# Cosine attention and an MLP mixer on one core: two row sums move from VectorE to GpSimd, and one block of queued matmuls is queued a slot later

## The chip, the cores and the metric

The kernel runs on one NeuronCore of a Trainium2 chip. The core has a matrix engine (TensorE; PE for its matmuls and PEld for its weight loads in the profile), VectorE (DVE), ScalarE (ACT), GpSimd (POOL) and SyncE (SP, which here only issues DMAs). Each engine runs its own instructions in the order in which the program lists them, and waits for the others through semaphores. The metric is the device time of one execution in microseconds (us); lower is better.

## The reference

Eight batches of attention over normalised queries and keys, and then, on the attention's output x, a token mixer and a channel mixer:

```python
# q, k, v: (8, 12, 448, 64)
q_n = q / (norm(q) + 1e-6);  k_n = k / (norm(k) + 1e-6)
attn = softmax(q_n @ k_n.T / tau)            # per batch and head, 448 x 448
x = (attn @ v)                               # -> (8, 448, 768)
h = relu(x.T @ w_tok1) @ w_tok2              # 448 -> 256 -> 448, over tokens
u = x + h.T
h2 = relu(u @ w_ch1) @ w_ch2                 # 768 -> 1536 -> 768, over channels
out = u + h2
```

## The kernel before, in words

**The main loop.** Twelve heads are taken in pairs, six pairs to a batch, so there are 48 pairs, numbered i = 0 to 47. One turn of the loop, called slot i here, carries several pairs at different stages: the scores and exponentials of pair i (`score`, L345, L352), the product with v of pair i-1 (`pv_rest`, `pv`, L367, L384, with the normalisation on VectorE, L387 and L388), the first token layer of pair i-1 (`tok1`, L420, its relu on VectorE, L423), the second token layer of pair i-2 (`tok2`, L434, its residual sum u on VectorE, L437) and the transposing DMA of that u into `ut` (`udma`, L443). The same slot casts v of pair i on GpSimd (`cast_v`, L228, L230), scales q and k of pair i+2 there (L298, L306), and sends them through a transposing DMA into `qk` (L330), all DMAs from SyncE's queue, in the program's order. An instruction that waits in a queue holds everything behind it.

**The channel layers are filler.** The channel mixer of the batches that are done is cut into units: one first-layer unit is six matmuls (`m_ch1`, L467, profile name psG; a batch has twelve), one second-layer unit is twelve matmuls (`m_ch2`, L483, psF). `refill(b)` appends a batch's units to a list; each slot adds an allowance (`fed[1]`, set by `RATES`) and takes units off the front until the allowance is used: one unit between `pv` and `score_rest`, the rest after `tok2`. For batch 5 (`KEPT_B`) the twelve first-layer units are put at the **front** of the list. Before the change that happens in slot 38, so that slot 38 takes two units of batch 5's first layer, slots 39 and 40 three each, slots 41 and 42 two each, and the unit of batch 4's second layer that stood at the front (psF of batch 4, block 0, second half) is taken in slot 42. A first-layer unit of batch 5 reads the transposed u of all six pairs of that batch, 30 to 35; u of pair 35 is made and sent in slot 37.

**The end is computed another way.** The second layer of batch 5 and both channel layers of batches 6 and 7 are left to the end and done with a seven-product scheme for 2 x 2 blocks (Strassen's, in Winograd's form). It needs sums and differences of blocks. Those of w_ch1 are `fast_weights1` (1 = s1w, 2 = s2w, 4 = s4w in the profile; 3 is written over a part of wc1t); s2w needs s1w, s4w needs s2w. Those of w_ch2 are `fast_weights2` (t1w, t2w, t3w, t4w, three parts each). Those of the activations are `fast_x` (t1x to t4x) for the first layer and `fast_g(g, k)` for the second, where g is one of five groups of rows and k = 1 to 4: the row sums S1 = G21 + G22 and S2 = S1 - G11, and so on. Group 0 is made of rows of batch 5 alone, so that its S1 and S2 (s1g and s2g) can be made before the loop ends. All of these are plain two-input fp16 operations (L536). S1 and S2 of group 0 are read first by `fast_g(0, 4)` and by the products `q5(0)` and `q6(0)` after the whole first layer.

**Where they stand before.** In slot 45 (NP_ALL - 3) VectorE's queue has, behind the relu of `tok1`, s1g and s2g, and behind these the reciprocals and products that finish the attention of pair 45 (`x`, L388). GpSimd's queue has in slot 46 the cast of v, s1w and t2w part 0; in slot 47 the cast of v, t2w part 1 and s4w; and then t4x's last part and t2w part 2. After the loop VectorE has `fast_weights1(3)` (wc1t, L536), t1x, then the sum u of pair 46 (L437).

Of the kernel before, what the change touches and what calls it, by code (L numbers as in the profile page):

```python
# [22 lines left out]
def kernel(  # L23
# [12 lines left out]
    nc = tc.nc  # L36

    B, H, S, E = q.shape
# [9 lines left out]
    NPAIR = H // 2  # L48
    NP_ALL = B * NPAIR
# [49 lines left out]
    def old(i):  # L99
        return i < OLD  # L100
# [167 lines left out]
    def norms(i, a0=0, a1=2, dve=False):  # L268
        st = pipe[i]
        n, sl = some(i, a0, a1)  # L270
        rn = st["rn"][0:n, sl]
        ne = nes[i % 3][0:n, sl]
        if dve:
            nc.vector.tensor_reduce(out=rn, in_=ne, axis=AXX.X, op=ALU.add)
            nc.vector.reciprocal(out=rn, in_=rn)  # L275
            return
        nc.scalar.activation(out=rn, in_=st["ssq"][0:n, sl], func=AF.Ln, bias=tiny[0:n])
        nc.scalar.activation(out=ne[:, :, 0], in_=rn, func=AF.Exp, scale=0.5)
# [59 lines left out]
    def score(i, c):  # L338
        n = SC if old(i) else 128
        qk = pipe[i]["qk"].rearrange("p a c s -> p (a c s)")  # L340
        qm = pipe[i]["qk"][:, 1, :, 0:SC]
        psS = ps2.tile([128, 2, 512], FP32, name=f"psS_{i}_{c}", tag="s")
        for hh in range(2):
            hb = slice(hh * 64, hh * 64 + 64)
            nc.tensor.matmul(psS[:, hh, 0:S], qk[hb, c * n:c * n + 128], qm[hb], start=True, stop=True)  # L345
        nc.scalar.activation(out=pts[i % 2][0:n, 2 * S * c:2 * S * (c + 1)].rearrange("p (h s) -> p h s", h=2),  # L346
                             in_=psS[0:n, :, 0:S], func=AF.Exp, scale=inv_tau)
# [77 lines left out]
    def tok2(i, pe=False, wide=False):  # L425
        st = pipe[i]
        b, pj = i // NPAIR, i % NPAIR
        if pj == 0:
            u16[b] = mix.tile([128, DT, 4, 128], FP16, name=f"u16_{b}", tag="u16", bufs=4)
            ut[b] = mix.tile([128, DT, 4, 128], FP16, name=f"ut_{b}", tag="ut")  # L430
        psU = (ps2 if wide else ps).tile([128, 4, 128], FP32, name=f"psU_{i}", tag="s" if wide else "b")
        for m, lo in enumerate(windows(b)):
            for tt in range(TT):
                nc.tensor.matmul(psU[:, m], w2t[:, tt, lo:lo + 128], st["rt"][:, tt],  # L434
                                 start=(tt == 0), stop=(tt == TT - 1))
        u = u16[b][:, pj]
        nc.vector.tensor_tensor(out=u, in0=psU[:], in1=st["x"][:], op=ALU.add)  # L437
        if not pe:
            udma(i)
# [5 lines left out]
    def upose(i, n=1):  # L445
        b, pj = i // NPAIR, i % NPAIR
        psT = ps.tile([128, n, 4, 128], FP16, name=f"psT_{i}", tag="b")
        for j in range(n):
            for m in range(4):
                nc.tensor.transpose(psT[:, j, m], u16[b][:, pj + j, m], id16[:])  # L450
        nc.vector.tensor_copy(out=ut[b][:, pj:pj + n], in_=psT[:])


    def upose_act(i, wide=False):
        psT = (ps2 if wide else ps).tile([128, 4, 128], FP16, name=f"psT_{i}", tag="s" if wide else "b")
        for m in range(4):
            nc.tensor.transpose(psT[:, m], u16[0][:, i, m], id16[:])
        nc.scalar.activation(out=ut[0][:, i], in_=psT[:], func=AF.Copy)
# [73 lines left out]
    KEPT_B = B - 3  # L532
    fw = {}

    def tt(eng, out, a, b, op):
        eng.tensor_tensor(out=out, in0=a, in1=b, op=op)  # L536
# [15 lines left out]
    def fast_weights1(n, eng):  # L552
        s, w = fw["s"], w1part
        out, a, b, op = {1: (s[0], w(1, 0), w(1, 1), ALU.add), 2: (s[1], s[0], w(0, 0), ALU.subtract),
                         3: (w(1, 0), w(0, 0), w(1, 0), ALU.subtract), 4: (s[2], w(0, 1), s[1], ALU.subtract)}[n]
        tt(eng, out if n == 3 else out[:], a[:] if n == 2 else a, b[:] if n == 4 else b, op)
# [87 lines left out]
    def fast_weights2(n, parts=range(3)):  # L644
        def w(i, j):
            return [wc2t[:, HC * i + 2 * m:HC * i + 2 * m + 2, DH * j:DH * (j + 1)] for m in range(3)]

        t = fw.setdefault("t2", {})
        if n not in t:
            at = [(n - 1 + m) % 2 for m in range(3)]  # L650
            t[n] = [qkv.tile([128, 2, DH], FP16, name=f"t{n}w2_{m}", tag=("qf", "kf")[z]) for m, z in enumerate(at)]
        a, b = {1: (w(0, 1), w(0, 0)), 2: (w(1, 1), t.get(1)), 3: (w(1, 1), w(0, 1)), 4: (w(1, 0), t.get(2))}[n]
        for m in parts:
            tt(nc.gpsimd, t[n][m][:], a[m], b[m] if n % 2 else b[m][:], ALU.subtract)
# [11 lines left out]
    def gtile(t, i):  # L666
        g, at = (gts["new"], t - 3) if 3 <= t < 7 else (gts[KEPT_B // 2], t if t < 3 else t - 3)
        return g[:, HC * i:HC * (i + 1), 128 * at:128 * at + 128]

    def s_tile(g, k):  # L670
        if g == 0 and k < 3:
            return qkv.tile([128, HC, 128], FP16, name=f"s{k}g_0", tag=("qf", "kf")[k - 1])[:]
        if g % 2:
            return xtile(k, f"g_{g}", [128, HC, 128])[:]
        n, part = (2, k - 3) if g == 0 else (1, k - 1) if k < 4 else (2, 4 - g)
        if n not in fw["room"]:
            fw["room"][n] = room(n, [128, 3, HC, 128], FP16)
        return fw["room"][n][:, part]

    def fast_g(g, k):  # L680
        r1, r2 = TILES[g]
        s = sg.setdefault(g, {})
        s[k] = s_tile(g, k)
        a, b, op = {1: lambda: (gtile(r2, 0), gtile(r2, 1), ALU.add),
                    2: lambda: (s[1], gtile(r1, 0), ALU.subtract),
                    3: lambda: (gtile(r1, 0), gtile(r2, 0), ALU.subtract),
                    4: lambda: (gtile(r1, 1), s[2], ALU.subtract)}[k]()
        tt(nc.vector, s[k], a, b, op)

    def prod2(n, g, out, start, lo=0, hi=DH):  # L690
        r1, r2 = TILES[g]
# [90 lines left out]
        return queue and fed[0] > queue[0][0] / 2  # L782

    KEPT = 6000.0
    RATES = {2 * NPAIR + 2: 4350.0, NP_ALL - 10: 3200.0}
    ACT_SQ = range(NP_ALL - 10, NP_ALL - 3)

    def refill(b):
# [7 lines left out]
    with tc.manual_schedule():  # L796
# [145 lines left out]
        for i in range(NPAIR + 1, NP_ALL):  # L942
            b, pj = i // NPAIR, i % NPAIR
            for c in range(KC):
                score(i, c)
                if c == 1 and NP_ALL - 6 <= i < NP_ALL - 2:
                    norms(i + 2)
            if i == NPAIR + 1:
                upose(i - 4, 2)
                tok2(i - 2, pe=True)  # L950
                pv_wide(i - 1)
                upose_act(i - 2)
                x_wide(i - 1)
                sums(i + 2)
            else:
                pv_rest(i - 1)
                pv(i - 1, 0)
                pv(i - 1, 1)
            if i == NP_ALL - 1:
                fast_weights1(2, nc.vector)  # L960
            if i == NPAIR + 1:
                refill(0)
            elif pj == 2 and 1 < b < B - 1:
                refill(b - 1)
            side(i)
            fed[1] = RATES.get(i, fed[1])
            if i == NP_ALL - HP:
                fed[1] = (sum(t for t, _ in queue) - fed[0]) / HP
            fed[0] += fed[1]
            unit(True)  # L970
            if old(i):
                score(i, KC)
            else:
                score_rest(i)
            if i in ACT_SQ:
                square(i + 3, 1, act=True)
            if i > NPAIR + 1:
                tok2(i - 2)
            if i + 1 < DMA_T0:
                tpose(i + 1)  # L980
            if due():
                unit(True)
            while due():
                unit()
            tok1(i - 1)
            if i + 3 < NP_ALL:
                sums(i + 3)
            if NP_ALL - 6 <= i < NP_ALL - 3:
                fast_weights2(1, (i - NP_ALL + 6,))
            if i == NP_ALL - 3:  # L990
                fast_g(0, 1)
                fast_g(0, 2)
                early.close()
                tail = ctx.enter_context(tc.tile_pool(name="tail", bufs=1, side="right", reuse_waits="tile"))
                tail_tiles()
            if i == NP_ALL - 2:
                fast_weights1(1, nc.gpsimd)
                fast_weights2(2, (0,))
            if i == NP_ALL - 1:
                fast_weights2(2, (1,))  # L1000
                fast_weights1(4, nc.gpsimd)
        last = NP_ALL - 1
        while queue:
            unit(True)
# [94 lines left out]
        g = n - 1  # L1099
# [46 lines left out]
```

## Time and profile before

| what | value |
|---|---|
| time, three runs | 394.35, 396.0, 394.37 us; median 394.37 |
| the profiled execution's own time | 392.86 us |
| its span, first to last instruction | 391.1 us |
| mean granted TensorE clock | 0.985 |
| matmuls of the first channel layer (L467) | 432, 89.5 us busy |
| matmuls of the second channel layer (L483) | 432, 76.2 us busy |
| s1w and s4w on GpSimd (128 x 2304, fp16) | 4.54 us each |
| t1w, t2w, t3w, t4w, one part (128 x 768, fp16) | 1.63 to 1.64 us where nothing is in the way |
| s2g on VectorE (128 x 768, fp16) | 0.56 us |
| s2w and wc1t on VectorE (128 x 2304, fp16) | 1.35 us each |

A page of the profile shows one execution: busy time of each engine, the span in forty slices, and the chain of work that ended last, followed back from the last instruction to what released each one. A line of the chain or of a timeline reads: start in us from the span's beginning, length in us, engine, what it writes, line of the program, how many. In timelines the form out<-in with shapes follows, and in square brackets the engine's idle time before and what ended it. A VectorE or GpSimd instruction's length includes time in which it has been issued and cannot proceed; a wait for a semaphore shows as idle time before it.

### The profile page before, as it was taken

Reading aid. Unit: us, or ns where it says so; the run is one execution under the profiler, and the core shown is the slowest. Engines: PE = TensorE matmul, PEld = TensorE weight load, DVE = VectorE, ACT = ScalarE, POOL = GpSimd, SP = SyncE. Lnnn points to the kernel's source line nnn. Section 1 sums busy time; section 2 is a strip of 40 time slices with the busy share of each in tenths; the row PEclk is TensorE's granted clock in tenths of the full one; section 3 lists DMA queues with packets and bytes.
Section 4 is the critical chain, followed back from the end, with each engine's and each line's share of the span. In section 5 each row is a group of like instructions: output and inputs, shape, how many; then the busy total and the mean of one; then the engine's idle time right before and its main releaser. Section 6 shows DMA issues by size and latency. Waiting matters only on the chain.

```text
span 391.1 us, 10297 instructions
## 1 busy us (share of the span) xinstructions
PE 367.7 (94%) x4074; PEld 240.6 (62%) x4074; DVE 260.6 (67%) x567; ACT 238.0 (61%) x412; POOL 288.0 (74%) x415
## 2 busy tenths in 40 slices
PE   7788999999999999999999999979999579999993
PEld 6466666676666666667667666646666356556662
DVE  7789866675646674566536675446667978797872
ACT  5999877665774456844866448758877324355110
POOL 8999988878767667668677667654789914797752
PEclk9999999999999999999999999999999959999999
DMA  7999999969997979767988899658797602103244
GB/s 211 278 226 241 260 228 217 178 147 220 208 213 141 215 171 213 172 151 193 186 204 142 208 195 209 163 136 154 183 176 156 109 13 55 22 0 91 82 139 105
DMA packets 118064, 64.65 MB, mean 165 GB/s; under 512 B 74240, under 2 KB 114560, under 8 KB 118016
## 3 DMA queue, kind: packets, MB, share of 16 engines
q1 hardware_dynamic: 111984, 58.42, 68.0%
q0 software_dynamic: 5616, 5.21, 8.5%
q8 instruction: 32, 0.52, 0.6%
q10 hardware_dynamic: 416, 0.36, 0.3%
q14 instruction: 16, 0.13, 0.1%
HBM read 43.45 MB, written 11.01 MB: 139 GB/s over the span
## 4 chain that ended last, share of the span: by engine, by line
PE 83%; DVE 6%; DMA 6%; ACT 1%; POOL 1%; issue 1%; SPq 0%; DVEq 0%; POOLq 0%
PE psG L467 20%; PE psF L483 18%; PE psO L384 9%; PE psS L345 7%; PE psU L434 5%; PE psR L420 5%; PE psYo L695 4%; DMA qf<-in_q_dram 3%; PE psY L590 3%; PE psZo L695 2%; PE psXo L695 2%; DVE s1g L536 2%; DMA kf<-in_k_dram 2%; PE psX L590 2%; PE psZ L590 2%; PE psQ L352 2%
## 5 line engine op out<-in xcount | busy, mean ns | idle before, releaser
L346 ACT ACTIVATE pt<-psS 128x896 f16<-128x896 f32 (+1 forms) x156 | 132.8, 916 | 57.6 <-PE psS L345 57.5
L467 PE MATMUL psG<-ut,wc1t 128*128 128x448 f16 x432 | 89.5, 352 | 2.4 <-DMA ut<-u 2.4
L298 POOL TENSOR_TENSOR kq<-kf,rn 128x384 f16<-128x384 f32 (+1 forms) x47 | 41.8, 890 | 62.4 <-DVE rn L275 58.8
L483 PE MATMUL psF<-wc2t,gt 128*128 128x384 f16 x432 | 76.2, 328 | 0.0
L467 PEld LDWEIGHTS <-wc1t 128*128 128x128 f16 x432 | 39.7, 98 | 31.0
L266 DVE TENSOR_REDUCE ssq<-sq 128x15 f32<-128x960 f32 (+2 forms) x51 | 56.1, 1101 | 2.9 <-ACT sq L248 1.9
L470 ACT ACTIVATE gt<-psG 128x448 f16<-128x448 f32 x72 | 38.7, 538 | 28.3 <-PE psG L467 28.3
L483 PEld LDWEIGHTS <-gt 128*128 128x128 f16 x432 | 40.7, 98 | 24.7 <-issue 0.7
L298 POOL TENSOR_TENSOR kq<-qf,rn 112x512 f16<-112x512 f32 x45 | 47.0, 1044 | 3.0
L423 DVE TENSOR_SCALAR rt<-psR 128x256 f16<-128x256 f32 x48 | 20.0, 418 | 41.7 <-PE psR L420 41.6
L345 PE MATMUL psS<-qk 64*128 64x448 f16 x312 | 42.4, 361 | 3.9 <-DVE qk L324 3.0
L487 DVE TENSOR_TENSOR ost<-psF,u 128x384 f32<-128x384 f32 (+1 forms) x42 | 22.8, 542 | 29.6 <-PE psF L483 29.4
L250 POOL TENSOR_TENSOR sq<-kf 128x384 f32<-128x384 f32 (+1 forms) x46 | 40.1, 873 | 0.0
L384 PE MATMUL psO<-vt,pt 128*128 128x65 f16 (+1 forms) x1024 | 39.7, 195 | 0.0
L434 PE MATMUL psU<-rt,w2t 128*128 128x128 f16 x384 | 29.8, 221 | 7.8 <-DVE x L388 7.3
L384 PEld LDWEIGHTS <-pt 128*128 128x128 f16 (+1 forms) x1024 | 34.7, 98 | 3.5 <-issue 0.9
L388 DVE TENSOR_TENSOR x<-psO,rec 128x256 f16<-128x256 f32 x82 | 34.8, 424 | 2.8
L437 DVE TENSOR_TENSOR u<-psU,x 128x512 f16<-128x512 f32 x48 | 32.2, 670 | 4.8 <-PE psU L434 3.5
L434 PEld LDWEIGHTS <-w2t 128*128 128x128 f16 x384 | 25.0, 99 | 15.6 <-DVE x L388 7.7
L250 POOL TENSOR_TENSOR sq<-qf 112x512 f32<-112x512 f32 x32 | 33.2, 1039 | 0.0
L420 PEld LDWEIGHTS <-w1t 128*128 128x128 f16 x384 | 25.2, 99 | 7.9 <-issue 1.8
L420 PE MATMUL psR<-x,w1t 128*128 128x128 f16 x384 | 29.8, 221 | 0.2 <-DVE u L437 0.2
(139 smaller groups left out, 532.1 us busy)
## 6 DMA issues: line engine op xcount, KB each, us to landing
qf<-in_q_dram SPq DMA_DIRECT2D x47, 224.0 KB, 4.2
kf<-in_k_dram SPq DMA_DIRECT2D x36, 192.0 KB, 3.9
vf<-in_v_dram SPq DMA_DIRECT2D x36, 192.0 KB, 3.6
vf<-in_v_dram SPq DMA_DIRECT2D x12, 224.0 KB, 7.6
kf<-in_k_dram SPq DMA_DIRECT2D x11, 224.0 KB, 7.8
wc1t<-in_moe_w_ch_dram POOLq DMA_DIRECT2D x4, 576.0 KB, 10.4
wc2t<-in_moe_w_ch_dram POOLq DMA_DIRECT2D x2, 1152.0 KB, 12.2
out_dram<-ost SPq DMA_DIRECT2D x5, 336.0 KB, 3.4
```

Source lines behind the costliest of these rows:

```text
L250: nc.gpsimd.tensor_mul(out=dst, in0=src, in1=src)
L266: nc.vector.tensor_reduce(out=st["ssq"][0:n, sl], in_=st["sq"][0:n, sl], axis=AXX.X, op=ALU.add)
L298: eng.tensor_tensor(out=kq[0:p, a, 0:n].rearrange("p c g e -> p g c e"), in0=st["kq"[a]][:].rearrange("p (g c) e -> p g c e", g=2), in1=_b ...
L345: nc.tensor.matmul(psS[:, hh, 0:S], qk[hb, c * n:c * n + 128], qm[hb], start=True, stop=True)
L346: nc.scalar.activation(out=pts[i % 2][0:n, 2 * S * c:2 * S * (c + 1)].rearrange("p (h s) -> p h s", h=2), in_=psS[0:n, :, 0:S], func=AF.Ex ...
L384: nc.tensor.matmul(psO[:, m, 0:E + 1], pts[i % 2][0:n, at:at + 128], vt[0:n, i % HP, nch * hh + c, 0:E + 1], start=(old(i) and c == 0), st ...
L388: nc.vector.tensor_tensor(out=st["x"][:, :, hh * E:(hh + 1) * E], in0=psO[:, :, 0:E], in1=_bcast_free(rec[:], E), op=ALU.mult)
L420: nc.tensor.matmul(psR[:, tt], w1t[:, w1[m], tt * 128:(tt + 1) * 128], st["x"][:, m], start=(m == 0), stop=(m == 3))
L434: nc.tensor.matmul(psU[:, m], w2t[:, tt, lo:lo + 128], st["rt"][:, tt], start=(tt == 0), stop=(tt == TT - 1))
L467: nc.tensor.matmul(psG[:, 0:S], wc1t[:, dt, ct * 128:(ct + 1) * 128], ut[b][:, dt].rearrange("p m s -> p (m s)")[:, lo:lo + S], start=(dt ...
L470: nc.scalar.activation(out=gt[:, ct, (b % 2) * S:(b % 2 + 1) * S], in_=psG[:, 0:S], func=AF.Relu)
L483: nc.tensor.matmul(psF[:, 0:hi - lo], gt[:, ct, at:at + 128], wc2t[:, ct, lo:hi], start=(ct == 0), stop=(ct == CT - 1))
```

## The change

Three edits. The first-layer units of batch 5 are put to the front of the list in slot 39 in place of 38, and the allowance per slot from 38 on is 3100 in place of 3200. `fast_g` takes an engine, and S1 and S2 of group 0 go to GpSimd, in slot 47, between the last cast of v and s4w. Part 0 of t2w moves from slot 46 to slot 45, and part 1 from before s4w to behind it.

```diff
-    def fast_g(g, k):
+    def fast_g(g, k, eng=nc.vector):
...
-        tt(nc.vector, s[k], a, b, op)
+        tt(eng, s[k], a, b, op)
...
-    RATES = {2 * NPAIR + 2: 4350.0, NP_ALL - 10: 3200.0}
+    RATES = {2 * NPAIR + 2: 4350.0, NP_ALL - 10: 3100.0}
...
-            elif pj == 2 and 1 < b < B - 1:
+            elif pj == (3 if b - 1 == KEPT_B else 2) and 1 < b < B - 1:
                 refill(b - 1)
...
             if i == NP_ALL - 3:
-                fast_g(0, 1)
-                fast_g(0, 2)
+                fast_weights2(2, (0,))
                 early.close()
...
             if i == NP_ALL - 2:
                 fast_weights1(1, nc.gpsimd)
-                fast_weights2(2, (0,))
             if i == NP_ALL - 1:
+                fast_g(0, 1, nc.gpsimd)
+                fast_g(0, 2, nc.gpsimd)
+                fast_weights1(4, nc.gpsimd)
                 fast_weights2(2, (1,))
-                fast_weights1(4, nc.gpsimd)
```

With the new allowance the list is taken off as follows (G is a first-layer unit of batch 5, F a second-layer unit of batch 4): before, slots 38 to 43 take 2 G, 3 G, 3 G, 2 G, 2 G + F, F; after, F, 3 G, 3 G, 2 G, 3 G, G + F. From slot 44 on both take the same units. The two stores of F's rows to memory move with it on SyncE's queue, from behind slot 42 to behind slot 38. GpSimd's order at the end becomes: scaling of pair 47, t2w part 0, cast, s1w, cast, s1g, s2g, s4w, t2w part 1, t4x's last part, t2w part 2; from there on it is as before.

## The prediction

> **What bounds the kernel now.** I read the page's engine shares first, then the chain of waits in order of time, then the two places where the chain leaves TensorE late in the run.
>
> ```profile
> PE 367.7 (94%) x4074; PEld 240.6 (62%) x4074; DVE 260.6 (67%) x567; ACT 238.0 (61%) x412; POOL 288.0 (74%) x415
> ...
> 256.85 1.00 DVE ssq L266
> 257.85 3.46 DMA ut<-u
> 262.34 1.14 PE psG L467 x6
> ...
> 301.38 1.95 PE psF L483 x12
> 305.02 9.43 DVE s1g L536
> 315.64 1.03 PE psU L434 x8
> ```
>
> TensorE is the bound, so only its idle time and its clock are to be had. The two non-PE pieces are the two places that the change touches. Instruction by instruction:
>
> ```profile
> 304.94 9.50 DVE L536 TENSOR_TENSOR s1g<-gt 128x768 f16<-128x768 f16 x1
> ...
> 305.86 4.54 POOL L536 TENSOR_TENSOR s1w<-wc1t 128x2304 f16<-128x2304 f16 x1
> 310.35 1.63 POOL L536 TENSOR_TENSOR t2w<-wc2t,t1w 128x768 f16<-128x768 f16 x1
> ...
> 312.39 1.63 POOL L536 TENSOR_TENSOR t2w<-wc2t,t1w 128x768 f16<-128x768 f16 x1
> ...
> 345.99 1.63 POOL L536 TENSOR_TENSOR t4w<-wc2t,t2w 128x768 f16<-128x768 f16 x1
> 346.32 1.72 DVE L536 TENSOR_TENSOR room<-gt 128x768 f16<-128x768 f16 x1
> 347.60 1.95 POOL L536 TENSOR_TENSOR t4w<-wc2t,t2w 128x768 f16<-128x768 f16 x1
> ```
>
> s1g takes 9.50 us, its equal s2g 0.56. It ends at 314.44, 0.42 after GpSimd's last t2w (312.39 + 1.63 = 314.02). S3 (346.32 + 1.72 = 348.04) likewise ends 0.42 after the t4w part that ends at 347.62, and the next t4w part is stretched from 1.63 to 1.95. So a VectorE operation with two inputs in SBUF and GpSimd's two-input operations exclude each other. S3 got in between two GpSimd instructions; s1g was passed over at five ends of them. Both behaviours go into the bounds.
>
> ```profile
> core 0: us, PE busy (x) PEld busy (x) DVE busy (x) ACT busy (x) POOL busy (x), PEclk, DMA share, GB/s
> 260.02:263.42 3.40, 2.07 (x18) 1.33 (x18) 0.85 (x2) 1.50 (x3) 2.98 (x6) 1.00 0.18 29
> 307.81:311.21 3.40, 0.54 (x4) 0.10 (x1) 3.40 (x1) 0.54 (x1) 3.40 (x2) 1.00 0.80 193
> 311.22:315.64 4.42, 0.00 (x0) 0.00 (x1) 4.35 (x5) 0.00 (x0) 2.81 (x3) 0.50 0.00 0
> 315.64:321.45 5.81, 5.81 (x58) 4.22 (x59) 4.06 (x11) 2.54 (x3) 0.00 (x0) 0.50 0.12 23
> ```
>
> Behind the row sums TensorE is idle for 7.30 us (308.35 to 315.64) and the granted clock is 0.50 from 311.22 to 321.45, 10.2 us. The 2.37 us wait for the transposed u at 259 to 261.35 brought no drop. All sums below are against this execution: span 391.1, time 392.86, which is 1.51 under the median of the runs; that difference I don't add. About 0.5% is what a measurement of this kernel can tell from no change.
>
> **Part 1, the later refill.** In slot 38 the first G starts at 257.88 and would take 1.13; its last matmul runs at 261.35 instead of 258.82, so the wait costs 2.53. After the change one F (1.95) stands there in place of two G (2 x 1.13), and slot 39 begins at 263.85 - 2.53 - 0.31 = 261.0; the 0.31 comes back later, as work. The first G now follows pv in slot 39, at 262.6, and u has landed (257.85 + 3.46 = 261.31): 1.3 us to spare. What comes next is SyncE's queue:
>
> ```profile
> 262.94 1.23 SPq L330 DMA_TRANSPOSE qk<-kq  x1
> ...
> 267.58 1.23 SPq L443 DMA_TRANSPOSE ut<-u  x1
> 270.49 1.23 SPq L330 DMA_TRANSPOSE qk<-kq  x1
> ...
> 276.97 1.23 SPq L330 DMA_TRANSPOSE qk<-kq  x1
> ```
>
> The transposes at 262.94 wait for GpSimd's scaling, which hangs on the exponentials of slot 38 and comes no earlier. A transpose lands 3.1 us (median) to 4.5 us after its issue in this stretch. Pair 40 is wanted at 267.1 and lands from 266.0 (the one before took until 267.3): a wait of 0 to 0.3. Behind it the queue runs without a gap, and now carries F's two stores as well, about 1.05 us (such a pair took 0.98 at 233.12 and 1.55 at 306.81). So u of pair 36 goes at 268.6 and qk of pair 41 at 269.8 (0.6 earlier than before, while TensorE is 2.85 earlier); qk of pair 42 follows 6.48 later, at 276.0 (270.49 to 276.97 was contiguous), and lands at 279.1 to 280.5, wanted at 278.5. Slot 42 thus starts 0.6 to 2.0 late. Slots 43 and on have slack again (SyncE then waits for scaling, until 282.76). Part 1 gives 2.5 less 0.6 to 2.0: **0.5 to 1.9**, taken as 1.8, since 3.1 is the landing of transposes issued back to back.
>
> **Part 2, the row sums.** The instants below leave part 1 out; it shifts all engines alike. Without s1g, VectorE finishes x of pair 45 at 307.2, in time for tok2 at 308.18. From the end of psF (308.15) to the pv of pair 46 I take the 2.49 us between the same two in slot 47 (322.95 to 325.44): two half-height sums, u, relu. So pv 310.64, the next psU 313.54, against 322.97 before: 9.4 us gained so far, 7.3 of idle time and the rest the clock.
>
> Then it is given back. GpSimd ends the scaling of pair 47 at 305.45, then t2w 1.6, cast 0.45, s1w 4.54 (to 312.0), cast 0.45 (312.4), s1g and s2g: 2 x 1.64 by t1w of the same size, and 0.08 since s2g waits for s1g. VectorE is done with x of pair 46 at 312.5 and its next is s2w (1.35), which needs what GpSimd holds. s4w needs s2w and s2g. In whatever order the two engines get in, s1g, s2g, s2w (1.22 once admitted) and s4w (4.54) stand in one row: 312.4 + 3.36 + 1.22 + 4.54 = 321.5. Behind s4w stand t2w (1.63) on GpSimd and on VectorE wc1t (1.22) and t1x (0.75), again exclusive: if wc1t goes first, t2w goes before t1x; if not, wc1t and t1x follow t2w. Either way t1x ends near 325.0, and u of pair 46 (0.69) at **325.65**. TensorE needs it for `upose(last - 1)`, 330.50 before: a gain of 4.85 there. The relu and the fast_x pieces behind u then run tighter on VectorE (rt to the last u took 3.0 us before), some 0.5 later than TensorE would like: 4.3 by the end, where TensorE alone sets the pace (psZo, psYo, psXo, 0.97 each). S1 and S2, ready by 317, are wanted after 345; the t2w parts too.
>
> TensorE's idle time in this stretch is spread by the order of admission: s2w at once, about 0.3 before pv of pair 47 and 4.5 before upose; between s1g and s2g (my choice, because s2g really waits there), 1.7 and 2.9; behind s2g, 3.4 and 1.2.
>
> **The clock** is the term that I can't read off. Idle stretches of 2.37 and 7.30 us bound it: the first brought no drop (least busy 3.4 us window: 2.07), the second did (0.54 busy). 2.9 to 4.5 lies between, nearer by its upper half to the second. If it drops, up to 10.2 us run at half speed, of which TensorE works about 9.5: 4.8 lost, the 0.5 above no longer counts, and part 2 gives 4.85 - 4.8, some **0 to 1**, taken 0.3. If not, **4.3**.
>
> The Trainium skill, "TensorE: Matmul & The Clock Gate", Part 1, says that the clock halves after at least one idle window of about 3.4 us of a free-running count. The trace agrees in kind, though its window had 0.54 us of work. By the page's rule alone a 2.9 us wait drops nothing, and the sum would be 4.3. The skill's "SBUF — State Buffer", Who interferes with whom, speaks against putting more two-input work on GpSimd: a VectorE instruction with two SBUF inputs and a GpSimd instruction that reads SBUF block each other, and the loser waits for the one instruction. S3 fits that, s1g (five instructions) doesn't. By the page s2w is admitted at 312.45, by the s1g row not before 314.0; the end of the chain, 325.65, is the same.
>
> **The sum.** 392.86 - 1.8 - 0.3 = **390.7 us**, with the clock dropping once more.
>
> **The rivals.**
> - *No clock drop* (25%): the idle time falls in two pieces, neither filling a window. 392.86 - 1.8 - 4.3 = 386.8.
> - *No exclusion in the new place* (8%): s2w and wc1t find the gaps and TensorE meets no wait before upose, 321.1 against 330.5: 392.86 - 1.8 - 9.4 = 381.7. Against it: every overlap of this kind in the trace shows the 0.42 ending.
> - *Part 1 does nothing* (12%): the wait for u becomes an equal wait for qk of pair 42 (landing 4.5 after issue, 0.5 left), with the drop in part 2: 392.86 - 0.5 - 0.0 = 392.4.
> - *Slower* (10%): the same queue, worse. If qk of pair 42 comes 2.9 us late or more (issue to landing 5.4, against 4.5 at most here), TensorE's clock halves in slot 42 as well: 2.9 + 10.2 / 2 = 8.0 lost against 2.5 and 0.3 gained: 398.
> - The forecast has 45%; its own range is 389.9 (392.86 - 1.9 - 1.0) to 392.4.
>
> **How the numbers follow.** The range runs from just under the no-drop case to just above the case in which part 1 gives nothing: 385.5 to 393.5; it leaves out the 8% below and the 10% above. Faster by over 0.5% means under 392.4: most of the forecast (40), no drop (25), no exclusion (8) = 0.73. Same: the rest of the forecast (5) and most of the nothing case (10) = 0.15. Slower 0.12.
>
> **What would show it.** Right: no DMA piece near 258 in the chain; TensorE working through 308 to 315; s2w or wc1t on VectorE stretched to several us beside s1g, s2g, s4w; an idle stretch of 2.5 to 4.5 us on TensorE shortly before the transposes of psT; a granted clock of 0.50 for some 10 us after it. Wrong: s2w and wc1t at 1.35 us, or the clock at 1.00 throughout, or score waits in slots 40 to 42 over 2 us.

## The result, and the profile after

| | before | after |
|---|---|---|
| median of the timed runs | 394.86 us (394.23 to 396.13) | 388.80 us (387.51 to 390.43), 6 runs |
| ratio, with its 95% interval | | 0.9845 (0.9811 to 0.9878) |
| the profiled execution's own time | 392.86 us | 388.35 us |
| its span, mean granted clock | 391.1 us, 0.985 | 386.6 us, 0.999 |

The change makes the kernel 1.5% faster, 6.1 us by the medians and 4.5 us between the two profiled executions; the prediction said 390.7 us, in 385.5 to 393.5. Where the difference between 6.1 and 4.5 may come from is taken up behind the last experiment.

The page of after, busy time and the granted clock in forty slices:

```profile
PE 365.5 (95%) x4074; PEld 238.9 (62%) x4074; DVE 255.7 (66%) x565; ACT 238.5 (62%) x412; POOL 293.8 (76%) x417
...
PEclk9999999999999999999999999999999999999999
```

TensorE has the same 4,074 matmuls and is busy 2.2 us less; no slice is left with a lowered clock. The chain of waits of after, in order of time, at the two places of the prediction:

```profile
262.30 0.67 PE psS L345 x6
263.24 0.85 PE psO L384 x24
264.09 1.14 PE psG L467 x6
...
270.94 4.83 DMA qk<-kq
275.81 0.74 PE psS L345 x6
...
312.68 2.95 DVE s2w L536
...
319.69 2.50 DVE wc1t L536
322.19 0.58 issue
322.77 2.28 DVE t1x L536
```

The transfer of u near 258 is gone: the first G of batch 5 now follows the pv of slot 39 at once. In its place stands a transfer of q and k at 270.94, that of pair 41. At the end s1g has gone, and the chain goes through three other VectorE operations of the same kind. TensorE's own timeline shows what each costs, in the square brackets (three lines of it, each behind a wait):

```profile
275.81 0.74 PE L345 MATMUL psS<-qk 64*128 64x448 f16 x6 [1.09 <-DMA qk<-kq]
...
317.46 0.61 PE L367 MATMUL psO<-vt,pt 64*128 64x65 f16 x8 [1.38 <-DVE u L437]
...
325.71 0.40 PE L450 MATMUL psT<-id,u 128*128 128x128 f16 x4 [2.49 <-DVE u L437]
```

Waits of 2.37 and 7.30 us have become 1.09, 1.38 and 2.49. Each of the last two lies behind a sum u, which lies behind two-input work that VectorE and GpSimd did one after the other, as their timelines show. GpSimd's timeline of after:

```profile
312.77 1.64 POOL L536 TENSOR_TENSOR s1g<-gt 128x768 f16<-128x768 f16 x1
314.49 2.63 POOL L536 TENSOR_TENSOR s2g<-s1g,gt 128x768 f16<-128x768 f16 x1
317.08 4.54 POOL L536 TENSOR_TENSOR s4w<-wc1t,s2w 128x2304 f16<-128x2304 f16 x1
321.59 2.75 POOL L536 TENSOR_TENSOR t2w<-wc2t,t1w 128x768 f16<-128x768 f16 x1
```

and VectorE's:

```profile
312.68 2.95 DVE L536 TENSOR_TENSOR s2w<-s1w,wc1t 128x2304 f16<-128x2304 f16 x1
...
319.69 3.15 DVE L536 TENSOR_TENSOR wc1t<-wc1t 128x2304 f16<-128x2304 f16 x1
322.77 2.28 DVE L536 TENSOR_TENSOR t1x<-ut,ut 128x1344 f16<-128x1344 f16 x1
324.98 0.68 DVE L437 TENSOR_TENSOR u<-psU,x 128x512 f16<-128x512 f32 x1
```

s2w, 1.35 us where nothing is in the way, takes 2.95 and ends at 315.63, 1.22 after s1g's end (312.77 + 1.64 = 314.41); s2g, issued at 314.49, is held up by it in turn and takes 2.63. wc1t ends 1.22 after s4w, t1x 0.7 after t2w. That is the predicted row: s1g, s2w, s2g, s4w, wc1t, t2w, t1x, u.

**Where the time came from.** Slot by slot, from TensorE's first score matmul of each slot (before / after, us):

| stretch | before | after | gained |
|---|---|---|---|
| start of the run to slot 38 | 256.30 | 257.54 | -1.24 |
| slot 38 to slot 39 | 7.55 | 4.69 | 2.86 |
| slot 39 to slot 46 | 40.49 | 42.46 | -1.97 |
| slot 46 to the transposes of u of pair 46 | 26.16 | 21.02 | 5.14 |
| those transposes to TensorE's end | 54.54 | 54.81 | -0.27 |

The sum is 4.52. The first row is no effect of the change: up to slot 38 the programs are the same, and 0.84 of it is a wait for a transposing DMA at 84.40 that the profile of before doesn't have. The views by windows, of slot 46 to the transposes in after:

```profile
304.69:316.07 11.38, 11.05 (x142) 7.41 (x141) 8.37 (x16) 6.17 (x8) 11.22 (x7) 1.00 0.44 84
316.07:317.46 1.39, 0.01 (x2) 0.03 (x2) 1.33 (x4) 0.92 (x1) 1.39 (x2) 1.00 0.14 33
317.46:323.23 5.77, 5.62 (x66) 3.57 (x65) 4.85 (x7) 1.84 (x2) 5.77 (x2) 1.00 0.35 83
323.23:325.71 2.48, 0.00 (x0) 0.00 (x1) 2.48 (x3) 0.92 (x1) 1.10 (x1) 1.00 0.00 0
```

The clock (third number from the right) stays at 1.00 through both waits. TensorE is busy 16.68 of these 21.02 us; before it was busy 18.86 of 26.16. So of the 5.14 us, 3.0 are idle time and 2.2 are matmuls that before ran at half clock.

### The profile page after: what moved, and what is told of

Its sections match the earlier page's. It is cut to its first block, busy times and chain, and to the rows that moved or that the text cites. A ratio compares the mean times of both kernels' runs of the same rounds, so it can differ in the third digit from the quotient of the medians.

```text
span 386.6 us, 10294 instructions
## 1 busy us (share of the span) xinstructions
PE 365.5 (95%) x4074; PEld 238.9 (62%) x4074; DVE 255.7 (66%) x565; ACT 238.5 (62%) x412; POOL 293.8 (76%) x417
## 4 chain that ended last, share of the span: by engine, by line
PE 77%; DMA 9%; DVE 8%; POOL 2%; ACT 1%; issue 1%; SPq 0%; DVEq 0%; POOLq 0%
PE psG L467 19%; PE psF L483 17%; PE psO L384 9%; PE psS L345 7%; PE psU L434 4%; PE psYo L695 4%; PE psR L420 4%; DMA qk<-kq 4%; DMA qf<-in_q_dram 3%; PE psY L590 3%; PE psZo L695 3%; PE psXo L695 2%; DMA kf<-in_k_dram 2%; PE psQ L352 2%; PE psZ L590 1%
## 5 line engine op out<-in xcount | busy, mean ns | idle before, releaser
L345 PE MATMUL psS<-qk 64*128 64x448 f16 x312 | 41.5, 355 | 6.4 <-DVE qk L324 3.0
```

## The experiments

Times are medians of five rounds unless said; the ratio is to the kernel before on the same chip. In the diffs the base is named.

**1. The change again** (no edit), so that it stands on the same chip as the variants:

> The changed kernel once more, for the spread of its executions beside the other three of this call. Theory (clock): the waits of 1.4 and 2.5 us near 316 and 323 make the TensorE clock drop in some executions and not in others; executions with a mean granted clock of 0.995 or more have spans of 385.5 to 386.7 us, those at 0.990 or less 387.3 to 388.7. Rival (transfers): spread comes from when DMAs land, and clock and span go together no more closely than by chance.

388.51 us, ratio 0.9817 (0.9784 to 0.985). Its waits are 1.16, 1.37 and 2.49 us, slot 46 to the transposes 21.01. The 1.16 is again for pair 41; pair 42 is waited for too, 0.34 us, which after did not show. In this execution TensorE's clock was halved for 6.83 us at 11.6, in the run's first microseconds, and not at the two waits: the stretch from slot 46 to the transposes repeats to 0.01 us, the start of the run doesn't. Clock and span do go together over the six executions (0.994 and 0.995: 385.6 to 386.6 us; 0.986: 387.4 and 387.5), but in this profile not through the waits that the theory named.

**2. The refill alone** (base: before):

```diff
-    RATES = {2 * NPAIR + 2: 4350.0, NP_ALL - 10: 3200.0}
+    RATES = {2 * NPAIR + 2: 4350.0, NP_ALL - 10: 3100.0}
...
-            elif pj == 2 and 1 < b < B - 1:
+            elif pj == (3 if b - 1 == KEPT_B else 2) and 1 < b < B - 1:
```

> The kernel before with the later refill and the allowance alone. Theory (SyncE's queue gives part of it back): the wait of 2.4 us for the transposed u goes, a wait of 1.0 to 1.5 us for qk of pair 41 comes, slot 38 to slot 46 is 0.7 to 1.2 us shorter, the time 0.5 to 1.5 us under the kernel before. Rival (the prediction's own term): wait at pair 42 and 1.8 us gained; other rival: all 2.5 us kept, or nothing gained.

392.07 us, ratio 0.9926 (0.9898 to 0.9954): 3.2 us under before's 395.3. In its profile slots 38 to 46 take 46.66 us, 1.38 less than before, with the new wait at slot 41 (0.95 us; the transposing DMA issued at 270.29 landed 4.69 later). The medians fell by more than the 0.5 to 1.5 us that were expected. The 7.30 us wait at the end is untouched, but the half clock at it lasted 6.83 us in place of 10.24, so slot 46 to the transposes took 25.04 us in place of 26.16.

**3. The row sums alone** (base: after, with the two lines above put back):

> The kernel before with the row sums on GpSimd and the moved t2w parts alone. Theory: the wait of 7.3 us goes, waits of about 1.4 and 2.5 us come, no drop of the clock in the tail; 4.5 to 5.5 us under the kernel before, and with the refill alone the two gains add up to that of the whole change within 1 us. Rival: the parts need each other, since part 1 shifts the tail against the transfers: under 3.5 or over 6.5 us.

389.71 us, ratio 0.9857 (0.9828 to 0.9887): 5.6 us. Slots 38 to 46 take 48.09 us as before (48.04), slot 46 to the transposes 21.00. By the profiles the two parts give 1.4 and 5.2 in their own stretches. The row sums leave the refill's stretch as it was; the refill leaves the wait in the row sums' stretch as it was, and what it gained there (1.1 us) is the shorter half clock of that one execution. By the medians the parts give 3.2 and 5.6, 8.8 together, against 6.1 and 6.9 for the whole. Each of these has an interval of over 1 us on both sides; the medians do not meet the expected sum within 1 us, and that the parts add up rests on the profiles.

**4. A filler in the two new waits** (base: after). Matmuls of the identity that nothing reads, so that TensorE doesn't fall idle:

```diff
         p1(0)
+        warm(10, True)
         pv_rest(last)
...
         p2(1)
+        warm(38, True)
         upose(last - 1)
```

> The changed kernel with 10 idle matmuls (128 columns, result unread) before pv of the last pair and 38 before the transposes of pair 46, about 0.6 and 2.1 us of work put into the two waits. Clock theory: no execution drops, mean clock 0.995 or more in all, spans 385.5 to 386.9, median about 1 us under the changed kernel of this call. Rival (transfers): same spread and median as the changed kernel, within 0.4 us. Third (fillers are in the way): 0.5 us or more slower, with the clock at 1.00.

388.47 us, ratio 0.9826 (0.9791 to 0.9861): equal to after (388.51). The waits shrink to 0.81 and 0.37 us, and slot 46 to the transposes still takes 21.01. The theory's marks (clocks of 0.995 and more, 1 us gained) did not come: the clocks are 0.986 to 0.994, the times 387.93 to 390.49. A drop of the predicted size would have cost some 4 us in each execution, and keeping TensorE at work would have won them back; so that drop isn't there in most executions. A short one in some of them is not excluded by medians that are good to about 1 us. The same profile holds a drop at another place. TensorE waited 2.08 us at 83.77; two windows, before and after the clock fell:

```profile
82.63:86.04 3.41, 1.33 (x20) 0.99 (x19) 2.74 (x5) 0.54 (x1) 2.75 (x6) 1.00 1.04 246
86.04:89.45 3.41, 3.41 (x42) 2.35 (x39) 1.32 (x5) 2.94 (x5) 2.38 (x4) 0.50 1.26 179
```

A window of 3.41 us in which TensorE was busy 1.33 us was followed by one of the same length at 0.50. (In before, the second to fourth row of the prediction's windows, it was 0.54 us busy, then 10.2 us at 0.50.)

**5. One t2w part moved out of the row** (base: after). Part 0 goes ahead of the scaling of pair 47 instead of behind it, and GpSimd's order behind the last cast becomes t2w part 1, s4w, s1g, s2g:

```diff
             cast_v(i)
+            if i == NP_ALL - 3:
+                fast_weights2(2, (0,))
...
-                fast_weights2(2, (0,))
...
             if i == NP_ALL - 1:
+                fast_weights2(2, (1,))
+                fast_weights1(4, nc.gpsimd)
                 fast_g(0, 1, nc.gpsimd)
                 fast_g(0, 2, nc.gpsimd)
-                fast_weights1(4, nc.gpsimd)
-                fast_weights2(2, (1,))
```

> The changed kernel with GpSimd's order changed: t2w part 0 in the gap before the scaling of pair 47, t2w part 1 in front of s4w, and s1g and s2g behind s4w. Theory (one row of exclusive work): what stands in front of s4w sets when u of pair 46 is ready; with 3.3 us less there s2w ends within 1.5 us of x of pair 46, the transposes of pair 46 start 2.5 to 3.2 us earlier relative to slot 46, the wait before them is under 1 us, the time is 2 to 3.5 us under the changed kernel. Rival: the row sums now collide with VectorE's small t2x, t3x, t4x instructions and give it back: within 0.5 us of the changed kernel or slower.

386.02 us (384.47 to 386.84), ratio 0.9755 (0.9719 to 0.9791). All six executions lie under all six of after on the same chip (387.33 to 389.30). GpSimd's timeline:

```profile
310.17 1.65 POOL L536 TENSOR_TENSOR t2w<-wc2t,t1w 128x768 f16<-128x768 f16 x1
313.17 4.55 POOL L536 TENSOR_TENSOR s4w<-wc1t,s2w 128x2304 f16<-128x2304 f16 x1 [1.35 <-issue]
317.68 2.76 POOL L536 TENSOR_TENSOR s1g<-gt 128x768 f16<-128x768 f16 x1
```

and VectorE's:

```profile
311.68 1.35 DVE L536 TENSOR_TENSOR s2w<-s1w,wc1t 128x2304 f16<-128x2304 f16 x1
...
317.10 1.83 DVE L536 TENSOR_TENSOR wc1t<-wc1t 128x2304 f16<-128x2304 f16 x1
318.86 2.29 DVE L536 TENSOR_TENSOR t1x<-ut,ut 128x1344 f16<-128x1344 f16 x1
```

GpSimd is 0.14 us from the end of t2w when s2w is issued, and then stands idle until s2w is done (1.35 us in the brackets; the profile names no releaser there, but s4w reads s2w), so s2w takes the 1.35 us that it takes alone; s1g and s2g, which nobody wants before 345, stand behind s4w. Slot 46 to the transposes: 18.12 us against 21.02. TensorE's wait before them, expected under 1 us, is 1.18. This is what the order of the exclusive work cost in the changed kernel: 2.9 us at the transposes, 0.5 given back behind them (t2x on VectorE now meets s2g, 0.89 us for 0.38, and TensorE waits 0.60), 2.5 in the medians.

**6. Only s4w moved ahead of the row sums** (base: after):

```diff
             if i == NP_ALL - 1:
+                fast_weights1(4, nc.gpsimd)
                 fast_g(0, 1, nc.gpsimd)
                 fast_g(0, 2, nc.gpsimd)
-                fast_weights1(4, nc.gpsimd)
                 fast_weights2(2, (1,))
```

> The changed kernel with s4w put in front of s1g and s2g, nothing else moved. Theory (one row of exclusive work): u of pair 46 comes about 2.8 us earlier relative to slot 46; t2w part 1 then meets t2x and t3x and costs up to 1.6: 0.7 to 2.5 us under the changed kernel. Rival (the sum of exclusive work counts, not its order): the transposes of pair 46 start at the same distance from slot 46 as in the changed kernel, within 0.5 us, and the time is the same.

387.67 us (386.57 to 389.84), ratio 0.9808 (0.977 to 0.9846), 0.8 under after on the same chip, with overlapping executions. Slot 46 to the transposes is 18.11, as in experiment 5; but then t2w part 1, still behind the row sums, holds t3x on VectorE (1.82 us for 0.38), and TensorE waits 2.04 us before the next transposes. A gain of 2.9 at one place leaves 1.0 at TensorE's end when the next wait takes its place.

**7. t2w part 1 between s1g and s2g** (base: after, one execution only):

```diff
                 fast_g(0, 1, nc.gpsimd)
+                fast_weights2(2, (1,))
                 fast_g(0, 2, nc.gpsimd)
                 fast_weights1(4, nc.gpsimd)
-                fast_weights2(2, (1,))
```

> The changed kernel with t2w part 1 moved between s1g and s2g, in front of s4w, so that no GpSimd instruction there really waits for the one before it. Theory A (VectorE is admitted only where GpSimd has a real gap or nothing queued): s2w is held behind t2w and s2g too, and runs 4.5 us or more; the wait before pv of the last pair grows from 1.4 to over 3 us. Theory B (admitted at an end of an instruction that falls well after the request): s2w is admitted at the end of s1g and takes 2.9 us as in the changed kernel, then GpSimd's t2w is stretched by about 1.2 us, u of pair 46 comes no earlier than in the changed kernel.

389.72 us beside 392.81 for before. GpSimd's and VectorE's timelines, one after the other:

```profile
311.46 1.64 POOL L536 TENSOR_TENSOR s1g<-gt 128x768 f16<-128x768 f16 x1
313.05 1.64 POOL L536 TENSOR_TENSOR t2w<-wc2t,t1w 128x768 f16<-128x768 f16 x1
314.65 1.63 POOL L536 TENSOR_TENSOR s2g<-s1g,gt 128x768 f16<-128x768 f16 x1
317.63 4.54 POOL L536 TENSOR_TENSOR s4w<-wc1t,s2w 128x2304 f16<-128x2304 f16 x1 [1.35 <-DVE s2w L536]
```

```profile
311.37 6.13 DVE L536 TENSOR_TENSOR s2w<-s1w,wc1t 128x2304 f16<-128x2304 f16 x1
```

s2w was passed over at the ends of the cast that ran when it was issued (311.50), of s1g and of t2w and went in only behind s2g (314.65 + 1.63 = 316.28, and it ends 1.22 later), where GpSimd had to wait for s2w itself. In after, where s2g directly follows the s1g that it needs, s2w got in between the two. So theory A's row came. TensorE waited 4.57 us, and here its clock did fall: 0.50 for 6.83 us from 317.86; slot 46 to the transposes 23.87 us. A drop behind these waits was therefore possible, as the prediction had it, in another order of admission.

**8. VectorE's row sums, with GpSimd cleared** (base: before; 3 rounds). The row sums stay on VectorE and both t2w parts go behind s4w:

```diff
             if i == NP_ALL - 2:
                 fast_weights1(1, nc.gpsimd)
-                fast_weights2(2, (0,))
             if i == NP_ALL - 1:
-                fast_weights2(2, (1,))
                 fast_weights1(4, nc.gpsimd)
+                fast_weights2(2, (0, 1))
```

> The kernel before, row sums still on VectorE in slot 45, but t2w parts 0 and 1 moved behind s4w, so that GpSimd has cast, s1w, cast queued when s1g asks. Theory A (s1g waits until GpSimd has nothing queued): s1g ends 0.42 us after the last of these, near 311.3 in the time base of the kernel before, length 6 to 6.5 us, TensorE's wait 4 us. Theory B (it is admitted at the first end of an instruction): s1g ends near 305.9, under 1.5 us long, and there is no wait of TensorE there. Rival C (s1g's 9.5 us are its own and not GpSimd's doing): 9 us or more as before.

394.30 us (391.08 to 396.67), ratio 0.9986 (0.9956 to 1.0016): no gain that can be measured. s1g on VectorE takes 5.88 us instead of 9.50, up to the end of s1w (311.10), which it also can't get in front of; TensorE waits 3.85 us, and the clock is 0.50 for 3.41 us behind it. s1g got in before the last cast was done, so theory A has the length about right and the condition wrong. In the profile this edit alone shortens slot 46 to the transposes from 26.16 to 22.95 us, and 0.8 of that comes back behind them; the medians show 1.0 us, within the noise. Taking t2w out of s1g's way is thus a part of the gain at that place, and not enough: s1w alone keeps s1g out. Moving the row sums to GpSimd takes the VectorE side of the collision away.

**9. The F stores on another queue** (base: experiment 5). The two stores of F's rows, which with the later refill stand in SyncE's queue ahead of the transposes of slot 39, go to ScalarE's:

```diff
-                eng = nc.scalar if st and n == 0 else nc.sync
+                eng = nc.scalar if (st and n == 0) or (b == 4 and m == 0) else nc.sync
```

> The kernel with the row sums behind s4w and t2w earlier (e5_gap), and the two stores of batch 4's first rows issued from ScalarE's queue in place of SyncE's. Theory (SyncE's issue order makes qk of pair 41 late): its transpose is issued 1.0 us earlier, TensorE's wait in slot 41 falls from 1.2 to under 0.4 us, the time 0.5 to 1.0 us under e5_gap. Rival (the transpose lands late for lack of DMA bandwidth, whoever issues the stores): issue to landing stays at 4.5 us or more and grows by what the issue gains; wait and time unchanged.

385.68 us (385.33 to 386.00, 4 runs), ratio 0.9763 (0.9738 to 0.9787); level with experiment 5 (0.9755), under the 0.5 to 1.0 us that were expected. SyncE's timeline of after:

```profile
268.49 1.01 SPq L502 DMA_DIRECT2D out_dram<-ost  x2
269.60 1.24 SPq L443 DMA_TRANSPOSE ut<-u  x1
270.94 1.25 SPq L330 DMA_TRANSPOSE qk<-kq  x1
```

and of this kernel:

```profile
268.40 1.24 SPq L443 DMA_TRANSPOSE ut<-u  x1
269.82 1.23 SPq L330 DMA_TRANSPOSE qk<-kq  x1
```

The transposing DMA of pair 41 is issued 1.1 us earlier, lands 3.3 us after its issue instead of 4.8 (4.9 in experiment 5), and the wait at slot 41 is gone. Both changed at once, the place in the queue and the time to landing, so the theory has half of it. A wait of 0.53 us appears at the start of slot 39 instead, where an exponential on ScalarE stands behind the stores. Slots 38 to 46: 46.31 against 46.97, so 0.7 us in the profile and 0.3 in the medians, which were taken on different chips and are within their spread.

**10 and 11. A filler in the wait of the kernel before** (base: before), to price the clock there. The first stood in the wrong slot, one after the wait:

```diff
+            if i == NP_ALL - 1:
+                warm(90, True)
             if i > NPAIR + 1:
                 tok2(i - 2)
```

> The kernel before, with 90 matmuls of 128 columns of the identity (about 0.056 us each by the row in which 38 of them shortened a wait by 2.1 us, so some 5.0 us) put into TensorE's queue before the second token layer of pair 45 in slot 47, where it waits 7.30 us. They compute nothing that is used. The wait itself stays as long in all, since the row sum on VectorE still ends behind GpSimd's last t2w; only its idle part falls to some 2.3 us. Theory 1 (of the 5.14 us that the change gains between the start of slot 46 and the transposes of u of pair 46, 3.0 are idle time and 2.2 are TensorE's matmuls at half clock, 18.86 us busy before against 16.68 after): no granted clock under 1 behind the wait, and slot 46 to the transposes 24.0 us (23.5 to 24.6) in place of 26.16; the time 1.5 to 2.7 us under before. Theory 2 (the clock costs nothing there, since VectorE's and GpSimd's chain to u of pair 46 sets the transposes): a wait of 1 to 2 us before these transposes and 25.6 us or more, the time within 0.8 us of before's. If the spread of before's executions (granted clock 0.968 to 0.987) comes from this place, this kernel's clocks lie above 0.985 and its times spread by under 2 us; if it comes from elsewhere in the run, they spread as before's do.

399.22 us, ratio 1.0101 (1.0048 to 1.0154). The wait of 7.31 us and the clock drop behind it are as before; the 90 matmuls take 5.19 us where TensorE waits for nothing, and the stretch from slot 47 to the transposes is 4.6 us longer. So the run doesn't answer its question, and says only that TensorE has under 1 us of slack there. The second has NP_ALL - 2 in place of NP_ALL - 1:

> The kernel before with the same 90 matmuls, this time in slot 46, where the wait of 7.30 us is (the run before had them a slot later, where TensorE waits for nothing, and they cost 4.6 us there). The wait is filled but for some 2.1 us, and TensorE's matmuls of 5.2 us are work that nothing reads. Theory 1 (of the 5.14 us that the change gains between the start of slot 46 and the transposes of u of pair 46, 3.0 are idle time and 2.2 are TensorE's matmuls at half clock): no granted clock under 1 behind the wait, slot 46 to the transposes 24.0 us (23.5 to 24.6) in place of 26.16, the time 1.5 to 2.7 us under before. Theory 2 (VectorE's and GpSimd's chain to u of pair 46 sets the transposes whatever the clock): a wait of 1 to 2 us before them, 25.6 us or more, the time within 0.8 us of before's. If the spread of before's executions (granted clock 0.968 to 0.987) comes from this place, the clocks lie above 0.985 here and the times spread by under 2 us; if from elsewhere, they spread as before's do.

394.99 us (391.71 to 395.76, 12 runs), ratio 0.9991 (0.996 to 1.0023). In the profile the wait falls to 2.29 us, the clock holds at 1.00 behind it, and slot 46 to the transposes takes 24.62 us against 26.16, just beside the 24.6 at which the first theory's range ended. TensorE is busy 21.90 of these, 16.7 without the 5.19 of the filler, as in after (16.68): the full clock is worth the 2.2 us that subtraction gave. Filler and idle time together are 0.6 us longer than the old wait, so 1.54 are left, and a part of the second theory is true as well. The medians don't show it: 0.3 us, with an interval from 1.6 us less to 0.9 us more. The clocks of its 12 executions run from 0.979 to 0.996 and the times spread by 4 us, so the spread of before does not come from this place alone, if at all. The profile of this run shows another place where it can come from:

```profile
259.68 1.11 PE L467 MATMUL psG<-ut,wc1t 128*128 128x448 f16 x5
263.40 0.35 PE L467 MATMUL psG<-ut,wc1t 128*128 128x448 f16 x1 [2.62 <-DMA ut<-u]
...
263.78 1.02 PE L434 MATMUL psU<-rt,w2t 128*128 128x128 f16 x8
264.59 2.45 PE L467 MATMUL psG<-ut,wc1t 128*128 128x448 f16 x6
```

This is the wait for u of the transposing DMA in slot 38, the one that part 1 of the change removes. It was 2.37 us in the profile of before, and nothing followed. Here it is 2.62 us, and the eight psU behind it take 1.02 us instead of 0.61, the six psG 2.45 instead of 1.30: the clock was 0.50 from 263.81 for 3.41 us, and slot 38 took 9.47 us instead of 7.55. Experiment 10's profile has the same (3.11 us of waiting, 3.41 at half clock, 9.62 us).

## Why the prediction was right, and where it was off

**Direction and range.** Faster, with the chain as described; 388.8 lies 1.9 under the forecast of 390.7. From 392.86 the terms measured in the profiled execution are: part 1, 0.89 (forecast 1.8); part 2, 5.14 - 0.27 = 4.87 (forecast 0.3 with the clock drop, 4.3 without); and 1.24 lost at the start of the run, which no step had. 392.86 - 0.89 - 4.87 + 1.24 = 388.34, against 388.35. That the time lies in the range is owed to the range: it was drawn to take in the case without a drop. The forecast's own range, 389.9 to 392.4, does not hold 388.8, and the start of the run moved the figure towards it by luck.

**Part 1, first half: right.** Slot 38 was to become 2.85 us shorter, and became 2.86.

**Part 1, second half: the size was off, and the pair.** The prediction set 0.6 to 2.0 us of waiting at pair 42 and took 1.8 as the net, by a landing 3.1 us after the issue. The queue did what was said: the transpose of pair 41 was to go at 269.8, and went at 270.94 - 1.24 = 269.7 in before's time. But it landed after 4.83 us (4.69 in experiment 2), longer than the 4.5 that bounded the range, so TensorE waited 1.1 us at pair 41; pair 42, 3.17 us from issue to landing, then came just in time. (In experiment 1 it was 0.34 us late.) The 1.97 us given back from slot 39 to 46 are the 1.1 at pair 41, a wait of 0.15 for ScalarE, the 0.31 of work that was announced, and 0.4 in smaller pieces. Experiment 9 shows that the stores in the queue are behind it: with them elsewhere the wait is gone. Why a transposing DMA behind them also takes longer to land stays open.

**Part 2, the chain: right.** u of pair 46 was to be ready at 325.65, which is 21.3 us after the start of slot 46; the transposes that wait for it start 21.02 after it. The waits of 1.7 and 2.9 us were 1.38 and 2.49, in the order of admission that was chosen. What followed was to cost 0.5, and cost 0.27. Experiments 5 and 6 show that the chain is the cause: the same work in another order of GpSimd's queue shortens this stretch by 2.9 us.

**The clock: wrong, and the largest term.** This is the step that failed: "If it drops, up to 10.2 us run at half speed", taken as the likelier because 2.9 to 4.5 us were called nearer, by their upper half, to the 7.30 us that had brought a drop. That reading does not hold on its own numbers: halfway between 2.37 and 7.30 is 4.84, so all of 2.9 to 4.5 lies nearer to the wait without a drop. It didn't drop, in after or in its repetition, and filling the waits in experiment 4 gained nothing in the medians. The case at 25%, no clock drop (386.8), is what the profile shows.

The price was too high as well. 4.8 us supposed that TensorE works through 9.5 of 10.2 us at half clock; in before it worked 5.81 of them, and the half clock cost 2.2 us. Nor is a drop always 10.2 us long: 3.41 behind a wait of 3.85, 6.83 behind 4.57, and 10.24 or 6.83 behind 7.3. With the chosen waits a fair price would have been some 3.4 us at half clock, at most 1.7 lost.

What the runs show in place of the wait's length is a count that the prediction had beside it (2.07 and 0.54 us busy in a window). Within a trace, drops begin and end at whole multiples of 3.41 us from each other. Counted on in such windows from the edges that each trace shows, behind the first 20 us of the run, every window at full clock in which TensorE was busy 1.33 us or less was followed by half clock, and none in which it was busy 1.47 us or more was (1.47 and 1.48 in experiments 3 and 8, in slot 38). In after an edge falls at 324.29, inside the wait of 2.49 us, and the two windows were busy 2.35 and 1.99 us; in the repetition and in experiment 3 the wait was divided too. That was in part luck. In experiment 4 the edges lie 18.2 and 21.6 us behind the start of slot 46, and without its fillers the wait, 18.5 to 21.0 us behind it, would have fallen into one window with some 0.9 us of work. So a drop in other executions of after is to be expected by this count; no trace here shows one.

**The base: a point that was left open.** The prediction saw that the profiled execution was 1.51 us faster than the median and added nothing. The profiles of experiments 10 and 11 show one way in which other executions are slower: the 2.4 us wait for u in slot 38 makes the clock fall in some of them, at 1.3 to 1.7 us each beyond the longer wait (9.47 and 9.62 us for slot 38 against 7.55, less 0.25 and 0.74 of additional waiting). Part 1 removes this along with the wait, which agrees with the refill alone giving 3.2 us by medians and 1.4 in its stretch of the profile. The mean clocks do not single it out: they are 0.977 for before over 17 executions and 0.984 for the refill alone, but 0.991 for the change as a whole over 6 and just as much for the row sums alone over 5, which keep the wait in slot 38. How many executions of before have that drop wasn't counted, so its share of the difference between 4.5 and 6.1 us is argued, not shown; the start of the run, where drops of 3.4 to 6.8 us come and go, is part of it.

**The rivals.** No exclusion (381.7): fell, s2w, wc1t and t1x all show it. Part 1 nothing (392.4) and slower (398): fell, the wait at the queue was 1.1 us, under the 2.9 from which the second decided.

**A better version.** Experiment 5 beats both kernels, by 2.5 us against the change on the same chip and by 9.4 against before; experiment 9 adds nothing that its runs can tell.

## What to carry to other kernels

Moving work off an engine that waits pays only if the new place has room: here 2.9 us of the row sums' cost came along, because they were put ahead of the one GpSimd instruction that the chain needed, and putting them behind it was worth a further 2.5 us (with t2w out of the way as well). When two engines exclude each other, place the other engine's operation where GpSimd must wait for it anyway, and keep independent GpSimd work out of that stretch. A profile of one execution prices a wait, but whether the clock falls behind it differs from run to run with where the windows fall: before adding the clock to a sum, ask how little TensorE could work in any 3.41 us around the wait, price one window first, and look at several executions.

## What the runs showed of the hardware

- **Admission behind GpSimd has no simple order.** A VectorE operation with two inputs in SBUF ended 0.41 to 0.42 us (128 x 768) or 1.21 to 1.22 us (128 x 2304) after the GpSimd instruction that it waited for, but which instruction that is varies. s1g was passed over at five ends in before and at two in experiment 8, s2w at three in experiment 7 and at one in after; wc1t and t1x in after, and S3 in before, went in at the first. Some got in where GpSimd's next instruction had to wait for something (s2w in after and in experiment 7), others where it waited for nothing (wc1t in after, ahead of t2w; s1g in experiment 8, ahead of a cast), so that is not the rule, and the rule stays open. The Trainium skill, "SBUF — State Buffer", SBUF: two separate sides, has the one that starts second blocked for the other's whole instruction; the 9.50 and 6.13 us here are several.
- **The clock goes by windows of 3.41 us, and they need not be empty.** Drops in the middle of a run lasted 3.41, 6.83 or 10.24 us. Waits of 2.37, 2.42 and 2.49 us brought none in some profiles, 2.08, 2.62 and 3.11 did in others; TensorE's busy time in the window tells them apart in all traces here (1.33 us and less, a drop; 1.47 and more, none). At half clock it went on behind windows of up to 2.40 us busy and ended behind those of 2.75 and more. In the first 13 us of a run windows of 1.4 to 1.8 us busy were followed by a drop too, so busy time is not the whole rule. The Trainium skill, "TensorE: Matmul & The Clock Gate", Part 1, names a free-running window of about 3.4 us that has to be idle; the length agrees, the emptiness doesn't.
- **A transposing DMA landed 3.2 to 4.8 us after its issue** in the same stretch of one execution (pairs 42 and 41 of after), with equal sizes; the longer one stood directly behind two stores and another transpose.
- **GpSimd's s1g took 1.64 us** where VectorE's s2g of the same shape took 0.56, 2.9 times as long.
